# Causal attention, query blocks of 64, 128, 128 and 128 rows, scores as 64x64 products on four array quarters

## The chip, the core and the metric

The kernel runs on one core of a Trainium2 chip. The metric is device time in microseconds (us) of one execution; the lower the better. TensorE (PE in the rows; PEld is its weight load), VectorE (DVE), ScalarE (ACT), GpSimd (POOL) and SyncE (SP, which issues the DMAs) run their own instruction queues and meet at semaphores.

## What is computed

```python
def _attn_ref(q, k, v):                      # each (4, 12, 448, 64), float32
    scores = scale * np.matmul(q, k.transpose(0, 1, 3, 2))
    mask = np.triu(np.ones((seq, seq), dtype=bool), k=1)
    scores = np.where(mask, -1000000000.0, scores)
    scores = scores - np.max(scores, axis=-1, keepdims=True)
    attn = np.exp(scores)
    attn = attn / (np.sum(attn, axis=-1, keepdims=True) + 1e-09)
    return np.matmul(attn, v)

def _moe_ref(x, w_in, w_out, a, b):          # x: (1792, 768), d_ff 2048; w_in and w_out in float64
    h = x @ w_in
    P = a[0] + a[1]*h + a[2]*h**2 + a[3]*h**3
    Q = 1.0 + abs(b[0])*abs(h) + abs(b[1])*h**2
    return (P / (Q + 1e-6)) @ w_out
```

x is the attention output with heads side by side. The scores are causal: row r sees keys 0 to r.

## The kernel before

**Attention** goes over 24 head pairs p. The two heads of a pair lie on partition halves 0 to 63 and 64 to 127. A pair passes through these steps; a letter stands for each in the order tables:

- `ld`, `lv`: q, k and v by DMA (SyncE).
- `qk`: 16 transposes of q and k (TensorE); `qx`, `qy`, `kx`, `ky`: their eviction from PSUM to q and k tiles (ScalarE, four instructions; q is scaled by 1/8).
- `s.3` ... `s.0`: the scores of query blocks of 128 rows, the last of 64. Blocks 0 to 2 are one 64x128 product for each head (K is 64 rows, 128 columns of the array), in two PSUM tiles, one a head; the last, of 64 rows and 448 keys, is a 64x64 product a head into the two halves of one tile. The widths are 128, 256, 384 and 448 columns.
- `m.0` ... `m.6`: adds the mask and takes the negated row minimum of the negated scores (VectorE, one instruction and an accumulator read each); `e.0` ... `e.6`: exponential with row sum (ScalarE, an activation and an accumulator read); `r`: the reciprocal of the sums (VectorE, two instructions); `n.0` ... `n.6`: the scaling by it (GpSimd).
- `c.1`, `c.0`: 32 transposes of the result (TensorE), `a` and `v`: their eviction, the x = 0 half by ScalarE, the x = 1 half by VectorE.
- `d`: 12 PV products (TensorE); `dh`, `dl`: the high part of the output by ScalarE (xh), the rest by VectorE (xl).
- `cv.0` ... `cv.3`: a piece of the conversion of the float64 weights to float32, in turn on GpSimd (lines 135 and 139), VectorE (145, 150) and SyncE; it fills gaps and feeds the second stage.

What runs when is written out by hand: `ORDER` is one round of the pipeline, and `name@lag` takes the step for pair p - lag. In round p the scores of pair p, the normalisation of p - 1, the transposes and PV of p - 2 and the output of p - 3 go side by side. `HEAD`, `FIRST` and `TAIL` are the fill, round 0 and the end. Each engine's queue holds its steps in that order, and a queue's head that waits holds all behind it. PSUM for qk, s, c is a ring of three tile pairs (`ring`); a new user waits until the tile's old readers are done. s.0 shares the tiles of s.1.

**MoE** follows: 64 units of w_in products (line 203), the rational function, and w_out products (511, 512), in float32 split into a high and a low part.

Of the kernel before, what the change touches and what calls it, by code (L numbers as in the profile page):

```python
# [8 lines left out]
F32 = mybir.dt.float32  # L9
# [32 lines left out]
def kernel(  # L42
# [198 lines left out]
    def qk_pe(p):  # L241
        ps = psa[p] = [ring(x, "psA") for x in range(2)]
        for n, src in enumerate(("q", "k")):
            for c in range(NB):
                for x, w in enumerate((QB, CP - QB)):
# [3 lines left out]
                    )  # L249

    def cut(t, ps, x, n):
        lo, hi = x * QB, (QB, CP)[x]
        w = NB * (hi - lo)
        return (
            t.rearrange("p (c r) -> p c r", c=NB)[:, :, lo:hi],
            ps[x][:, n * w:(n + 1) * w].rearrange("p (c r) -> p c r", c=NB),
        )

    def q_ev(p, x):
        o, i = cut(Q[p % 2], psa[p], x, 0)  # L260
        nc.scalar.activation(out=o, in_=i, func=AF.Copy, scale=SCALE)  # L261

    def k_ev(p, x):
        if p not in K:
            K[p] = qk.tile([P, S], F32, tag="k", name="kt")
        o, i = cut(K[p], psa[p], x, 1)
        nc.scalar.copy(out=o, in_=i)
# [456 lines left out]
```

## Time and profile before

| | us |
|---|---|
| three runs, median (lowest to highest) | 639.85 (639.5 to 639.87) |
| the profiled execution | 638.61 |
| its span, first to last instruction | 636.5 |
| fill: to the start of pair 1's conversion step on VectorE | 19.01 |
| round 2 | 7.85 |
| rounds 3 to 22 | 122.87 |
| last round to the start of the w_out products | 26.73 |
| the rest of MoE | 460.04 |

The stages are cut at the start of VectorE's conversion step (line 145 or 150), which is the last VectorE step of a round. To read the profile: an engine's busy time in a stage says how full it is; the idle time before a group of instructions, and what ended it, says whom it waits for. A matmul row is one pass of a product, and a float32 product has two. Rows of one instruction have a duration that includes its latency, so the next one often starts before it ends; the distance from start to start is what an instruction costs its queue.

### The profile page before, as it was taken

What the parts mean: (1) busy time and instruction counts of PE and PEld (TensorE: products, weight loads), DVE (VectorE), ACT (ScalarE), POOL (GpSimd) and SP (SyncE); (2) the same over time, 40 slices, a digit from 0 to 9 for tenths busy, and PEclk for the clock granted to TensorE, in tenths of its full rate; (3) what the DMA queues carried; (4) which work ended last, traced back from release to release, by engine and by line L of the source; (5) the groups of instructions that cost most, each with busy time, mean ns of one, the idle gap of its engine ahead of it and who ended that gap; (6) DMA issues with size and microseconds to landing.
All of it is one profiled execution on the core that took longest, in us unless ns stands there. A gap on an engine that the chain in (4) does not pass through costs nothing.

```text
span 636.5 us, 12809 instructions
## 1 busy us (share of the span) xinstructions
PE 622.6 (98%) x4624; PEld 520.1 (82%) x4624; DVE 520.4 (82%) x1037; ACT 438.2 (69%) x989; POOL 179.1 (28%) x245
## 2 busy tenths in 40 slices
PE   7899999999999999999999999999999999999997
PEld 5566676666788887888888888889999999999996
DVE  2899999998699999999999868677875656885664
ACT  4899999998677766667777665554745465755453
POOL 2767777775643521113444100000000000000000
PEclk9899999999999999999999999999999999999999
DMA  8998889895268896888987987647477766667753
GB/s 182 225 222 191 205 226 205 194 258 180 61 223 298 290 362 239 306 303 288 325 309 286 323 306 278 226 148 271 177 235 249 254 228 225 222 199 248 248 198 125
DMA packets 109759, 151.84 MB, mean 239 GB/s; under 512 B 71040, under 2 KB 83328, under 8 KB 109696
## 3 DMA queue, kind: packets, MB, share of 16 engines
q1 hardware_dynamic: 109696, 151.02, 74.3%
q8 instruction: 37, 0.61, 0.4%
q14 instruction: 26, 0.21, 0.1%
HBM read 114.04 MB, written 36.96 MB: 237 GB/s over the span
## 4 chain that ended last, share of the span: by engine, by line
PE 90%; DVE 5%; ACT 2%; issue 1%; POOL 1%; ACTq 0%; DVEq 0%; POOLq 0%
PE psH L203 34%; PE psO L511 24%; PE psM L512 13%; PE psS L282 8%; PE psD L361 5%; PE psC L337 4%; PE psA L247 1%; DVE psS L295 1%; DVE at L347 1%; PE psI L614 1%; ACT e L302 1%; POOL e L317 1%; DVE xl L374 0%; DVE nm L295 0%; DVE p L471 0%
## 5 line engine op out<-in xcount | busy, mean ns | idle before, releaser
L203 PE MATMUL psH<-xh,whl 128*128 128x512 f32 (+1 forms) x768 | 175.8, 364 | 0.0
L511 PE MATMUL psO<-whl,gh 128*128 128x512 f32 x448 | 159.7, 392 | 1.6 <-ACT gh L477 1.1
L203 PEld LDWEIGHTS psH<-xh,whl 128*128 128x128 f32 x768 | 136.0, 188 | 15.3
L512 PE MATMUL psM<-whl,gh 128*128 128x256 f32 x448 | 126.2, 282 | 0.0
L455 ACT ACTIVATE u<-w,lnb 128x512 f32<-128x512 f32 (+1 forms) x64 | 43.0, 671 | 85.5 <-DVE w L440 85.5
L511 PEld LDWEIGHTS psO<-whl,gh 128*128 128x128 f32 x448 | 84.0, 188 | 20.2 <-ACT gh L477 2.2
L317 POOL TENSOR_SCALAR e<-e,r 128x384 f32<-128x384 f32 (+3 forms) x168 | 80.7, 502 | 38.5 <-DVE r L313 28.9
L302 ACT ACTIVATE e<-psS,nm 128x256 f32<-128x256 f32 (+3 forms) x168 | 83.6, 524 | 11.1 <-DVE nm L295 11.0
L203 PE MATMUL psH<-xl,whl 128*128 128x512 f32 (+1 forms) x384 | 87.4, 362 | 0.0
L512 PEld LDWEIGHTS psM<-whl,gh 128*128 128x128 f32 x448 | 84.5, 189 | 1.3
L295 DVE CUSTOM_DVE_ANT_0 psS<-psS,mask 128x128 f32<-128x128 f32 (+3 forms) x168 | 73.4, 473 | 11.7 <-PE psS L282 10.1
L511 PE MATMUL psO<-whl,gl 128*128 128x512 f32 x224 | 81.0, 390 | 0.0
L203 PEld LDWEIGHTS psH<-xl,whl 128*128 128x128 f32 x384 | 70.1, 188 | 7.5
L282 PE MATMUL psS<-kt,qt 64*64 64x448 f32 (+3 forms) x384 | 66.8, 457 | 1.4 <-ACT qt L261 1.2
L433 ACT ACTIVATE u<-psH 128x512 f32<-128x512 f32 (+1 forms) x64 | 34.5, 539 | 47.6 <-PE psH L203 47.5
L484 DVE TENSOR_TENSOR gl<-p,gh 128x384 fp32r<-128x384 f32 (+1 forms) x62 | 38.2, 617 | 35.0 <-ACT gh L477 35.0
L512 PE MATMUL psM<-whl,gl 128*128 128x256 f32 x224 | 63.2, 282 | 0.0
L135 POOL TENSOR_SCALAR u<-raw 128x768 f32<-128x768 f32 x32 | 37.4, 1170 | 85.6 <-DMA raw<-in_moe_w_in_dram 31.9
L186 DVE TENSOR_TENSOR whl<-w,whl 128x768 fp32r<-128x768 f32 x43 | 41.6, 968 | 22.6 <-ACT whl L178 22.2
L477 ACT CAST gh<-p 128x512 fp32r<-128x512 f32 (+1 forms) x64 | 36.8, 575 | 28.9 <-DVE p L471 28.9
L440 DVE SCALAR_TENSOR_TENSOR w<-w,bb,u 128x512 f32<-128x512 f32 (+1 forms) x64 | 48.2, 753 | 5.7 <-ACT w L434 5.7
L462 DVE SCALAR_TENSOR_TENSOR w<-w,u 128x512 f32<-128x512 f32 (+1 forms) x64 | 41.5, 648 | 10.2 <-ACT u L458 10.2
(62 smaller groups left out, 1028.8 us busy)
## 6 DMA issues: line engine op xcount, KB each, us to landing
whl<-whl SPq DMA_DIRECT2D x88, 768.0 KB, 4.2
w<-w SPq DMA_DIRECT2D x56, 384.0 KB, 5.1
raw<-in_moe_w_in_dram SPq DMA_DIRECT2D x16, 768.0 KB, 5.4
w<-u SPq DMA_DIRECT2D x32, 384.0 KB, 2.9
raw<-in_moe_w_out_dram SPq DMA_DIRECT2D x16, 768.0 KB, 5.4
qraw<-in_q_dram SPq DMA_DIRECT2D x48, 112.0 KB, 3.9
kraw<-in_k_dram SPq DMA_DIRECT2D x48, 112.0 KB, 4.1
out_dram<-osb SPq DMA_DIRECT2D x14, 384.0 KB, 2.8
```

Source lines behind the costliest of these rows:

```text
L186: eng.tensor_tensor(out=w[:, 1], in0=src, in1=w[:, 0].bitcast(F32), op=ALU.subtract)
L203: nc.tensor.matmul(ps, w[:, c * P:(c + 1) * P], x[c][:, lo:lo + n_tok], start=(c == 0 and n == 0), stop=(c == KD - 1 and n == 2),)
L282: nc.tensor.matmul(o if i < 3 else o[half(j)], Q[p % 2][half(j), i * P:min((i + 1) * P, S)], K[p][half(j), :w], start=True, stop=True, ski ...
L295: nc.vector.tensor_tensor_reduce(out=s, in0=s, in1=m, scale=-1.0, scalar=3e38, op0=ALU.add, op1=ALU.min, accum_out=nmx[p][:, i:i + 1],)
L302: nc.scalar.activation(out=E[p % 2][i][:, :w], in_=pss[p, i][1], func=AF.Exp, bias=nmx[p][:, i:i + 1], scale=-1.0, accum_out=SUM[p][:, i:i ...
L317: nc.gpsimd.tensor_scalar(out=e, in0=e, scalar1=REC[p][:, i:i + 1], scalar2=0.0, op0=ALU.mult, op1=ALU.add)
L440: nc.vector.scalar_tensor_tensor(out=w, in0=w, scalar=bb[:, 0:1], in1=u, op0=ALU.add, op1=ALU.mult)
L455: nc.scalar.activation(out=r, in_=w, func=AF.Ln, scale=2.0 ** -LSH, bias=lnb[:, 0:1])
L462: nc.vector.scalar_tensor_tensor(out=w, in0=w, scalar=QC, in1=r, op0=ALU.add, op1=ALU.mult)
L484: eng.tensor_tensor(out=gl, in0=pp, in1=gh.bitcast(F32), op=ALU.subtract)
L511: nc.tensor.matmul(acc[k], g, w[:, :512], start=first, stop=last)
L512: nc.tensor.matmul(m, g, w[:, 512:], start=first and k % 2 == 0, stop=last, skip_group_check=True)
```

## The change

- Query blocks are 64, 128, 128, 128 rows instead of 128, 128, 128, 64. The score widths become 64, 192, 320 and 448. Block 0 lies in one PSUM tile (two 64x64 products); each of the others is four 64x64 products, one for each half of the rows and each head, on the four quarters of the array. E tiles have 64 zeroed columns behind the scores where the block's transposes read past them.
- `qx`, `qy` evict q and k together, one instruction for each of the two PSUM tiles, into one `qkt` tile; for pairs 0 and 1 the second one is on VectorE. The scale 1/8 moves into the row-minimum instruction, and the mask values are divided by it.
- `c_pe` still has 32 transposes a pair, in another order of slots, so that `d` needs 8 products instead of 12.
- `ORDER`, `FIRST` and `TAIL` are new. After the first q and k transposes four more idle products (`keep_warm`) are issued, and the GpSimd part of the first weight conversion moves from round 0 to round 1.
- The masks are two tiles, and GpSimd fills the E tiles' zero columns at the start.

The core of the diff (of the order tables two lines):

```diff
-c.1@2 e.3@1 cv.3 qk@-1 lv e.0@1 v.1@2 dh@3 ld@-4 s.3 r@1 a.1@2 dl@3 n.5@1 qy@-1 c.0@2 m.6 kx@-1 n.4@1 ky@-1 s.2
+c.1@2 e.2@1 s.0 e.4@1 v.1@2 lv c.0@2 a.1@2 r@1 qk@-1 ld@-4 dh@3 v.0@2 n.4@1 s.3 cv.3 a.0@2 m.0 n.2@1 dl@3 qx@-1 n.6@1
...
+    def qk_ev(p, x):
+        if p not in QK:
+            QK[p] = qk.tile([P, 2, S], F32, tag="qk", name="qkt")
         lo, hi = x * QB, (QB, CP)[x]
+        o = QK[p].rearrange("p n (c r) -> p (n c) r", r=CP)[:, :, lo:hi]
+        i = psa[p][x][:, :2 * NB * (hi - lo)].rearrange("p (c r) -> p c r", r=hi - lo)
+        if p < 2 and x == 1:
+            nc.vector.tensor_copy(out=o, in_=i)
+        else:
+            nc.scalar.copy(out=o, in_=i)
...
-    b_w = (P, P, 2 * P, 2 * P, 3 * P, 3 * P, S)
+    b_w = (QB, 3 * QB, 3 * QB, 5 * QB, 5 * QB, S, S)
...
+        for n, j in ((0, 0), (1, 1), (1, 0), (0, 1)):
+            x = n if i else 1 - j
+            if i == 0 and n:
+                continue
+            r = (2 * i - 1 + (n + j) % 2) * QB if i else 0
+            nc.tensor.matmul(
+                ps[j][half(x), lo:lo + w], QK[p][half(j), 0, r:r + QB], QK[p][half(j), 1, :w],
+                start=True, stop=True, skip_group_check=True,
+            )
...
-            out=s, in0=s, in1=m, scale=-1.0, scalar=3e38,
+            out=s, in0=s, in1=m, scale=-SCALE, scalar=3e38,
...
     d_jobs = (
-        (0, 0, 0, 0, 0, 7), (1, 0, 0, 8, 0, 6), (1, 0, 0, 15, 6, 7),
-        (0, 1, 1, 0, 2, 7), (1, 1, 1, 8, 2, 6), (1, 1, 1, 5, 6, 7),
-        (0, 2, 1, 6, 4, 6), (1, 2, 1, 12, 4, 6), (0, 2, 1, 14, 6, 7), (1, 2, 1, 15, 6, 7),
-        (0, 3, 0, 14, 6, 7), (1, 3, 0, 7, 6, 7),
+        (0, 0, 0, 1, 0), (1, 0, 0, 8, 0), (0, 1, 1, 5, 2), (1, 1, 1, 0, 2),
+        (0, 2, 1, 13, 4), (1, 2, 1, 10, 4), (0, 3, 0, 15, 6), (1, 3, 0, 0, 6),
     )
...
-            lo = sum(quota(x) for x in range(p))
-            for m, n in steps[lo:lo + quota(p)]:
+            lo, hi = (sum(quota(x) for x in range(y)) for y in (0 if p == 2 else p, p + 1))
+            for m, n in steps[lo:hi]:
...
+        if p == 0:
+            keep_warm(4)
```

VectorE, the second part of a round: the row-minimum steps (`ISA psS,nm<-psS,mask`, with the width; the row behind each is its accumulator read), from the second copy of `at` on. Before:

```order
L347 COPY at<-psC 128x8x64 [waits PE_49]
L295 ISA psS,nm<-psS,mask 128x384 [waits PE_49]
L295 ISA nm 128x1
L295 ISA psS,nm<-psS,mask 128x384 [waits Activation_49]
L295 ISA nm 128x1
L295 ISA psS,nm<-psS,mask 128x128 [waits PE_49,Activation_49]
L295 ISA nm 128x1
L295 ISA psS,nm<-psS,mask 128x256 [waits DVE_49]
L295 ISA nm 128x1
L295 ISA psS,nm<-psS,mask 128x256 [waits PE_49]
L295 ISA nm 128x1
L295 ISA psS,nm<-psS,mask 128x128 [waits DVE_49]
```

Here the copy stands between the 448-wide step (just ahead of these rows) and the 384-wide ones. The same part of a round on VectorE after, from xl on:

```order
L379 TENSOR_TENSOR xl_86<-psD,xh_80 128x448 [waits Activation_49]
L299 ISA psS,nm<-psS,mask 128x448 [waits PE_49]
L299 ISA nm 128x1
L299 ISA psS,nm<-psS,mask 128x448
L299 ISA nm 128x1
L299 ISA psS,nm<-psS,mask 128x320 [waits PE_49,Activation_49]
L299 ISA nm 128x1
L299 ISA psS,nm<-psS,mask 128x192 [waits DVE_49]
L299 ISA nm 128x1
L299 ISA psS,nm<-psS,mask 128x320 [waits PE_49]
L299 ISA nm 128x1
L299 ISA psS,nm<-psS,mask 128x192 [waits DVE_49]
```

The copy of `at` and the new 64-wide step have moved ahead of xl. Both kernels have seven such steps a round, and in both two of them carry a wait on VectorE itself.

TensorE, the same round, the scores of the three wider blocks up to the first PV products (psS: scores, psD: PV). Before, they follow the last transposes of c:

```order
L337 MATMUL psC<-ident,e_214 128x64 x4
L282 MATMUL psS<-kt,qt_197 128x384 [waits Activation_49]
L282 MATMUL psS<-kt,qt_197 128x384 [waits DVE_49]
L282 MATMUL psS<-kt,qt_197 128x256 [waits PE_49,Activation_49]
L282 MATMUL psS<-kt,qt_197 128x256 [waits PE_49]
L282 MATMUL psS<-kt,qt_197 128x128 x2
L361 MATMUL psD<-at,vraw_199 64x448 [waits DMAHW3_49,DVE_49,Activation_49]
L361 MATMUL psD<-at,vraw_199 64x384 [waits DMAHW4_49]
L361 MATMUL psD<-at,vraw_199 64x64
L361 MATMUL psD<-at,vraw_199 64x320
```

The 448-wide products stand further up, behind the q and k transposes. The same place after; what stands ahead of these rows are the q and k transposes:

```order
L284 MATMUL psS<-qkt 64x448 [waits Activation_49]
L284 MATMUL psS<-qkt 64x448 [waits DVE_49]
L284 MATMUL psS<-qkt 64x448 x2
L284 MATMUL psS<-qkt 64x320 [waits Activation_49]
L284 MATMUL psS<-qkt 64x320 [waits DVE_49]
L284 MATMUL psS<-qkt 64x320 x2
L284 MATMUL psS<-qkt 64x192 x4
L366 MATMUL psD<-at,vraw_204 64x448 [waits DMAHW2_49,DVE_49]
L366 MATMUL psD<-at,vraw_204 64x448 [waits DMAHW3_49]
L366 MATMUL psD<-at,vraw_204 64x320 x2
```

The three wider blocks now follow each other in one go, four products each; the 64-column products (psS 64x64) have moved between the two groups of c transposes.

GpSimd, the fill, up to the normalisation of pair 0 (`e<-e,r`). Before:

```order
L610 MEMSET vraw_200 64x2x64
L135 TENSOR_SCALAR u<-raw_247 128x768 [waits DMAHW4_49,Pool_49]
L139 TENSOR_SCALAR raw_247<-raw_247 128x768 [waits Pool_49]
L317 TENSOR_SCALAR e_206<-e_206,r 128x384 [waits DVE_49,Activation_49]
L317 TENSOR_SCALAR e_205<-e_205,r 128x384 [waits Activation_49]
```

The conversion (L135, L139) is first. The same place on GpSimd after, behind the memsets of the E tiles:

```order
L621 MEMSET e_218 128x64
L324 TENSOR_SCALAR e_211<-e_211,r 128x320 [waits DVE_49,Activation_49]
L324 TENSOR_SCALAR e_209<-e_209,r 128x192
L324 TENSOR_SCALAR e_213<-e_213,r 128x448 [waits Activation_49]
L324 TENSOR_SCALAR e_207<-e_207,r 128x64
L324 TENSOR_SCALAR e_212<-e_212,r 128x448
L324 TENSOR_SCALAR e_210<-e_210,r 128x320
L324 TENSOR_SCALAR e_208<-e_208,r 128x192
L135 TENSOR_SCALAR u<-raw_263 128x768 [waits DMAHW4_49]
L139 TENSOR_SCALAR raw_263<-raw_263 128x768 [waits Pool_49]
```

The first conversion has moved behind the normalisation of pair 0.

## Rows read from the trace of the kernel before

**Rows 1.** The page: busy us (share) xinstructions; the chain's shares by engine.

```profile
PE 622.6 (98%) x4624; PEld 520.1 (82%) x4624; DVE 520.4 (82%) x1037; ACT 438.2 (69%) x989; POOL 179.1 (28%) x245
...
PE 90%; DVE 5%; ACT 2%; issue 1%; POOL 1%; ACTq 0%; DVEq 0%; POOLq 0%
```

**Rows 2.** Busy time by stage: start:end length, then PE PEld DVE ACT POOL, clock, DMA.

```profile
19.01:26.86 7.85, 7.64 (x86) 4.92 (x88) 6.06 (x22) 5.75 (x20) 5.69 (x10) 0.78 0.93 211
26.86:149.73 122.87, 122.74 (x1760) 82.78 (x1759) 119.94 (x404) 118.65 (x421) 88.52 (x158) 1.00 0.89 215
```

**Rows 3.** VectorE's groups, rounds 3 to 22: xcount | busy us, mean ns | idle before.

```profile
L295 DVE CUSTOM_DVE_ANT_0 psS<-psS,mask 128x384 f32<-128x384 f32 x40 | 21.4, 577 | 0.0
...
L295 DVE CUSTOM_DVE_ANT_0 psS<-psS,mask 128x256 f32<-128x256 f32 x40 | 16.3, 449 | 0.7
L295 DVE CUSTOM_DVE_ANT_0 psS<-psS,mask 128x128 f32<-128x128 f32 x41 | 12.9, 315 | 0.7
L295 DVE CUSTOM_DVE_ANT_0 psS<-psS,mask 128x448 f32<-128x448 f32 x20 | 12.5, 623 | 0.0
L374 DVE TENSOR_TENSOR xl<-psD,xh 128x448 fp32r<-128x448 f32 x20 | 12.0, 602 | 0.2
...
L313 DVE RECIPROCAL r<-sums 128x7 f32<-128x7 f32 x20 | 4.0, 201 | 1.4
```

**Rows 4.** Timeline of VectorE, inside one round: start us, us, instruction.

```profile
111.58 0.14 DVE L295 DVE_READ_ACCUMULATOR2_ANT nm<- 128x1 f32 x1
111.75 0.43 DVE L295 CUSTOM_DVE_ANT_0 psS<-psS,mask 128x256 f32<-128x256 f32 x1
```

**Rows 5.** Timeline of TensorE, one round, rows of one line merged.

```profile
101.19 0.41 PE L247 MATMUL psA<-ident,qraw 64*128 64x64 f32 x8
...
101.78 0.97 PE L282 MATMUL psS<-kt,qt 64*64 64x448 f32 x4
102.68 0.71 PE L337 MATMUL psC<-ident,e 64*128 64x64 f32 x16
103.22 1.70 PE L282 MATMUL psS<-kt,qt 64*128 64x384 f32 x12
104.85 1.98 PE L361 MATMUL psD<-at,vraw 128*64 128x448 f32 x24
106.76 0.46 PE L337 MATMUL psC<-ident,e 64*128 64x64 f32 x8
```

**Rows 6.** Timeline of ScalarE, the same round.

```profile
102.81 0.36 ACT L261 ACTIVATE qt<-psA 128x192 f32<-128x192 f32 x1
...
103.77 0.65 ACT L345 COPY at<-psC 128x512 f32<-128x512 f32 x1
104.23 0.72 ACT L302 ACTIVATE e<-psS,nm 128x448 f32<-128x448 f32 x1
104.76 0.28 ACT L302 ACTIVATION_READ_ACCUMULATOR e<-psS,nm 128x1 f32 x1
```

**Rows 7.** Timelines of TensorE, GpSimd and VectorE, the fill.

```profile
7.16 3.94 PE L282 MATMUL psS<-kt,qt 64*64 64x448 f32 x16 [1.23 <-ACT qt L261]
...
13.88 0.89 POOL L135 TENSOR_SCALAR u<-raw 128x768 f32<-128x768 f32 x1 [10.46 <-DMA raw<-in_moe_w_in_dram]
...
15.03 0.73 DVE L310 SCALAR_TENSOR_TENSOR sums<-sums 128x7 f32<-128x7 f32 x1 [1.83 <-ACT e L302]
...
16.16 3.36 POOL L317 TENSOR_SCALAR e<-e,r 128x384 f32<-128x384 f32 x7 [0.42 <-DVE r L313]
...
18.16 0.40 PE L337 MATMUL psC<-ident,e 64*128 64x64 f32 x6 [2.12 <-POOL e L317]
...
19.01 1.32 DVE L145 SCALAR_TENSOR_TENSOR u<-raw,u 128x768 uint32<-128x768 uint32 x1
```

**Rows 8.** Busy time and clock of a stretch of round 2, as in rows 2.

```profile
20.50:23.90 3.40, 3.40 (x24) 1.73 (x24) 2.08 (x6) 2.27 (x7) 2.50 (x6) 0.50 1.13 215
```

**Rows 9.** Timeline of TensorE, the end of attention.

```profile
155.04 1.98 PE L361 MATMUL psD<-at,vraw 128*64 128x448 f32 x24 [1.26 <-issue]
```

More of the change, by code (lines that the diff above doesn't have):

```diff
@@ L65 @@
     NP = B * HP
+    NE = 7
     SCALE = 1.0 / float(D) ** 0.5
@@ L249, in qk_pe @@
                     )
-    def cut(t, ps, x, n):
-        lo, hi = x * QB, (QB, CP)[x]
[L253 to L267, printed above, removed]
@@ L282, in stage_b_pe @@
             nc.tensor.matmul(
-                o if i < 3 else o[half(j)], Q[p % 2][half(j), i * P:min((i + 1) * P, S)], K[p][half(j), :w],
+                ps[j][half(x), lo:lo + w], QK[p][half(j), 0, r:r + QB], QK[p][half(j), 1, :w],
                 start=True, stop=True, skip_group_check=True,
             )
+        for j in range(2):
+            pss[p, max(2 * i - 1 + j, 0)] = ps[j][:, lo:lo + w]
     def stage_b_max(p, i):
         if p not in nmx:
-            nmx[p] = sm.tile([P, NQ], F32, tag="nm", bufs=2, name="nm")
@@ L359, in stage_d @@
         v = V[p % 3]
-        for j, c, h, slot, lo, hi in d_jobs:
+        for j, c, h, slot, lo in d_jobs:
             nc.tensor.matmul(
-                ps[half(j), lo * QB:hi * QB], v[:, j, c], a[h][:, slot * QB:(slot + hi - lo) * QB],
-                start=(c == 0 and lo == 0), stop=(c == 3), skip_group_check=True,
+                ps[half(j), lo * QB:S], v[:, j, c], a[h][:, slot * QB:(slot + 7 - lo) * QB],
+                start=(c == 0), stop=(c == 3), skip_group_check=True,
             )
@@ L577, with causal @@
         nc.gpsimd.memset(mask, 0.0)
-        nc.gpsimd.affine_select(
-            out=mask[:, 2 * P:3 * P], in_=mask[:, 2 * P:3 * P], compare_op=ALU.is_ge, fill=-1e9, base=0,
-            pattern=[[-1, P]], channel_multiplier=1,
-        )
-        for j in range(2):
-            m = mask[half(j), 3 * P + S - QB:]
+        nc.gpsimd.memset(mask0, 0.0)
+        def causal(m, base):
             nc.gpsimd.affine_select(
-                out=m, in_=m, compare_op=ALU.is_ge, fill=-1e9, base=0, pattern=[[-1, QB]], channel_multiplier=1,
-            )
+                out=m, in_=m, compare_op=ALU.is_ge, fill=-1e9 / SCALE, base=base, pattern=[[-1, m.shape[-1]]],
+                channel_multiplier=1,
+            )
+        causal(mask[:, 0, S - P:], 0)
+        for x in range(2):
+            causal(mask[half(x), 1, S - P:], QB - x * QB)
+            causal(mask0[half(x)], 0)
         es_l, es_r = ExitStack(), ExitStack()
@@ L610, with keep_warm @@
             nc.gpsimd.memset(V[x][:QB, :, 3], 0.0)
+        for x in range(2):
+            for e, w in zip(E[x], b_w):
+                if w < S:
+                    nc.gpsimd.memset(e[:, w:], 0.0)
         nc.vector.memset(warm, 0.0)
-        for _ in range(8):
-            nc.tensor.matmul(idle, warm, warm, start=True, stop=True, skip_group_check=True)
+        def keep_warm(n):
+            for _ in range(n):
+                nc.tensor.matmul(idle, warm, warm, start=True, stop=True, skip_group_check=True)
+        keep_warm(8)
         def attend(p, part):
```

70 lines of the change are left out of this document (36 added, 34 removed).

## The prediction

> **What bounds the kernel now.** I read the page's totals first. TensorE is busy 98% of the span and carries 90% of the chain [rows 1], so the first reading is "TensorE bounds everything, so every TensorE nanosecond saved counts". The change works in the attention stage only, so I cut the span there [rows 2]. The steady part of that stage is 26.86 to 149.73: 122.87 us for 20 rounds (one head pair each; the count is the x20 of xl in [rows 3]), 6.14 us a round. In it TensorE is busy 122.74 of 122.87, but VectorE is busy 119.94 and ScalarE 118.65 as well. Three engines are nearly full, and the question is which of them never waits for another.
>
> [Rows 3] answer it. The idle column of VectorE's groups adds up to 0.7 + 0.7 + 0.2 + 1.4 = 3.0 us in 122.87, and no group there has a releaser on another engine. The idle time is VectorE waiting for itself: [rows 4] show a row-minimum step whose scores lie in the same PSUM tile as the step before (the accumulator read starts at 111.58 and takes 0.14, the next step starts only at 111.75); the reciprocal waits for the sums. TensorE's rows, in contrast, can be full because it is held to VectorE's pace. So I take **VectorE as the bound of a round**, TensorE (6.1) and ScalarE just under it. Behind 176.46 nothing is changed.
>
> **The change, part by part.**
>
> *TensorE, scores.* Before, a round streams 448 columns in two 64x64 products at a time (101.78 to 102.68, 0.90 us) and 384 + 256 + 128 = 768 columns in two 64x128 products at a time (103.22 to 104.85, 1.63 us) [rows 5]: 2.01 and 2.12 ns a column, 2.53 us together. After, four products at a time stream 64 + 192 + 320 + 448 = 1024 columns. At the same two prices that is 2.06 to 2.17 us: 0.36 to 0.47 saved, if the four quarters really run at once. The trace of before shows pairs on row halves (768 columns) and on column halves (PV), each at full rate; it does not show four. *PV*: 12 products a pair become 8, with the same 1024 columns a head; 104.85 to 106.76 is 1.91 [rows 5], and I take 0 to 0.1 off. *Form changes*: s.0 now stands between two groups of transposes, so a round has five changes of tile form in place of four. The 448-column group has a change on both sides and yet costs less a column than the next group, which has none ahead of it, so a change is small: 0 to 0.1. TensorE's round falls by about 0.4, to 5.7.
>
> The Trainium skill, "TensorEngine Tiling (Array Packing)", Key Properties, says that changing the tiling mode drains TensorE, which speaks against a fifth change. By that rule the round would give back one drain; the trace shows none that stands out in the rows just named.
>
> *ScalarE.* Four evictions of q and k, 102.81 to 103.77, 0.96 us, become two of 512 and 384 elements; a 512-wide copy takes 0.65 with its latency [rows 6]. About 0.1 is saved. The exponentials keep their number (7) and their columns: 2(128 + 256 + 384) + 448 = 1984 before, 64 + 2(192 + 320 + 448) = 1984 after.
>
> *VectorE.* Also 7 row minima with 1984 columns. The four widths of [rows 3] lie on a line: 315, 449, 577 and 623 ns, about 1 ns a column on 185. Read off it, 64, 192 and 320 take 250, 380 and 510. Before: 2(0.577 + 0.449 + 0.315) + 0.623 = 3.305 us a round; after: 0.25 + 2(0.38 + 0.51 + 0.623) = 3.276. The instruction order keeps two self-waits a round (the two 192-wide steps that follow a 320-wide one in its tile). The copies, the sums, xl and the weight conversion are the same. So the bound engine saves 0.03 a round, and **the 0.4 saved on TensorE turns into idle time**. Over 20 rounds: -0.6. Bounds: if a 64-wide step costs as much as a 128-wide one, +0.065 - 0.03 a round, +0.7; if the idle of the reciprocal and of xl (1.4 + 0.2) is covered too, now that other work follows them, -2.2.
>
> Would TensorE's new order make VectorE wait? The last two exponentials of the previous pair (e.2, e.4) must free their PSUM tile before qk, and qk stands ahead of s.3. Counted from the conversion step that opens a round on VectorE: e.2 and e.4 are 192 and 320 wide, each below the 0.81 that a 448-wide one takes with its read (104.23 to 105.04 in [rows 6]), and end at about 1.2 (1.8 at most); qk takes 0.6 (101.19 to 101.78 in [rows 5]) and s.3 0.9, so s.3 ends at 2.7 (3.3 at most). VectorE needs it at about 3.2 (conversion 0.9, copy 0.6, sums and reciprocal 0.45, copy 0.6, first minimum 0.15, xl 0.5). That leaves 0.5, and nothing at the far end. SyncE's loads move by less than a step and still go out in the old sequence.
>
> *Fill.* Before, the first scores run from 7.16 to 11.1 (16 records, 3.94 us; the same 16 take 2.53 in a round, so TensorE was at its lower clock for part of it). The first sums wait for the last exponential until 15.03, the normalisation on GpSimd starts at 16.16 [rows 7], and the conversion of pair 1 on VectorE starts at 19.01 [rows 7], that of pair 2 at 26.86, where round 2 ends [rows 2]. After, q and k are evicted by two engines side by side, but four more warming products hold TensorE meanwhile: I start the scores at 7.2 again (0.4 either way). They take 3.94 x 1024/1216 = 3.3 at the old clock, 2.1 at the upper one; VectorE starts with the 64-wide block instead of the 448-wide, so behind the last score only the minima of 448, 320 and 448 and one eviction are left (about 2.0), then one exponential and its read (0.8 [rows 6], and 0.1 to start). The sums come at 10.5 + 2.0 + 0.9 = 13.4 (12.2 to 13.8), 1.6 earlier. Then a **give-back**: the first conversion on GpSimd (13.88 in [rows 7], ahead of the normalisation, when GpSimd had nothing to do) now stands behind it. Normalisation from about 14.2, 3.36 long, ends at 17.6; the conversion's first step needs 0.89 more; so VectorE's conversion of pair 1 starts at 18.5, only 0.5 earlier. Round 2 took 7.85 before, 1.7 above a later round, with TensorE at 0.50 of its clock, 1.2 GHz, from 20.5 to 23.9 [rows 8]; that stretch follows 2.12 us in which it waited for the normalisation [rows 7]. With scores and transposes further ahead I give that round 6.3 (5.6 to 7.85). So pair 2's conversion starts at 24.8 instead of 26.86: **-2.0**, bounds -0.2 and -3.8. The extra memsets and masks on GpSimd lie before 7 us, when nobody waits for it.
>
> *End.* Before, TensorE stands 1.26 us ahead of the PV products at 155.04, the last wait before the MoE products [rows 9]. The scores' buffers come free sooner and two PV stages shrink a little; 0 to -1.26, I take -0.4, near the small end, since the normalisation of pair 22 still has to end before the last transposes.
>
> **Sum.** -2.0 - 0.6 - 0.4 = -3.0. The profiled execution took 638.61 (span 636.5), so 635.6 for one like it; the median shown, 639.85, is 1.24 above it, so 636.9.
>
> **Rivals.**
> (a) *TensorE was the bound after all.* For it: 98% busy, 90% of the chain [rows 1]. Then 0.42 x 20 = 8.4 come off, and with fill and end 10.8: 629.0. Against it: VectorE's idle column. 0.08.
> (b) *The four quarters run two at a time* (the side of slower). The 960 columns of blocks 1 to 3 are then streamed twice: 960 x 2.1 ns = 2.0 us more, TensorE's round is 5.7 + 2.0 = 7.7, and it becomes the bound: 1.56 x 20 = 31, less 2.4 of fill and end: 668. It decides as soon as the scores cost 0.44 more than I reckon. For it: no row shows four. Against it: column halves and row halves each run in pairs at full rate. 0.07.
> The Trainium skill, "TensorE: Matmul & The Clock Gate", Part 3, reports that row and column packing compose; no run here shows that yet.
> (c) *The fill gives it all back*: the conversion of pair 1 behind the normalisation starts at 19.0 again, the half-clock stretch returns, the rounds end at 0 to +0.7 and the end at 0: 639.7 to 640.5, middle 640.1. For it: GpSimd's queue and the 7.85. 0.17.
>
> **Chances.** My forecast 0.68, rivals 0.08, 0.07, 0.17. The measurement tells about 0.2% (1.3 us) from no change. Faster: 0.64 of my forecast's 0.68 and all of (a), 0.72; same: 0.04 and most of (c), 0.16; slower: (b) and a part of (c), 0.12. The range reaches from 634.0 (fill and rounds near their good bounds) to 640.6 (rival c); (a) and (b) are left out.
>
> **What would show it.** VectorE's idle column in the rounds stays near 3 us with no other engine as releaser, and a round stays at 6.05 to 6.2; if it falls to 5.8, (a) is right. TensorE's busy share in the rounds falls to about 93%. The scores' groups take 2.1 us a round; near 4 would be (b). In the fill, the first sums at 13.4, the conversion of pair 1 at 18.5 with GpSimd as releaser, that of pair 2 at 24.8. I am wrong if VectorE waits for TensorE or ScalarE in every round, or if the conversion of pair 2 starts after 26.5.

## The result, and the profile after

The changed kernel takes 644.76 us (median of four runs, 643.4 to 645.2), the kernel before 639.86 beside it: a ratio of 1.0074, 95% interval 1.0057 to 1.0091. It is slower, where 636.9 us and faster were forecast. The profiled execution took 643.42 us, its span is 641.6 (before: 638.61 and 636.5). Printed intervals leave out executions that lie over 1.5% above the fastest of their kernel, and since some variants below spread over 2% by themselves, their lowest and highest times stand with them.

The page's totals, to set against [rows 1]:

```profile
PE 623.2 (97%) x4728; PEld 515.2 (80%) x4728; DVE 521.9 (81%) x1039; ACT 435.2 (68%) x939; POOL 178.9 (28%) x258
...
PE 77%; DVE 12%; POOL 3%; DMA 2%; ACT 2%; issue 2%; SPq 1%; DVEq 0%; ACTq 0%; POOLq 0%
```

The busy time has hardly moved. The chain has: VectorE carries 12% of it where it carried 5%, and GpSimd and the DMAs now carry 5% together, some 32 us, where GpSimd had 1%. The span cut by stage, as in [rows 2] (length, then busy PE, PEld, DVE, ACT, POOL, granted clock, DMA share, GB/s); a cut is again the start of VectorE's conversion step:

```profile
17.09:23.32 6.23, 5.59 (x80) 3.53 (x76) 6.07 (x22) 5.39 (x19) 4.11 (x8) 1.00 0.94 237
...
41.39:52.48 11.09, 7.93 (x104) 5.25 (x106) 6.29 (x22) 6.26 (x21) 7.73 (x15) 0.85 0.83 207
52.48:95.22 42.74, 42.05 (x643) 26.68 (x640) 41.75 (x141) 40.73 (x134) 31.05 (x56) 1.00 0.82 196
95.22:102.56 7.34, 6.21 (x104) 4.10 (x105) 6.21 (x21) 6.00 (x20) 4.71 (x9) 1.00 0.77 196
...
108.58:118.94 10.36, 7.85 (x94) 4.50 (x94) 6.60 (x21) 5.99 (x20) 6.51 (x13) 0.84 0.82 214
...
156.39:182.11 25.72, 24.98 (x222) 17.73 (x219) 18.56 (x39) 19.00 (x44) 15.26 (x19) 1.00 0.37 109
```

Round 2 (first row) starts 1.9 us earlier than before and is 1.6 shorter. The seven rounds from 52.48 take 6.11 each, as forecast. But three single rounds take 11.09, 7.34 and 10.36 us: 10.5 us above three of 6.1. The loss is these three rounds.

| | before | after |
|---|---|---|
| fill and round 2, to pair 2's conversion | 26.86 | 23.32 |
| 20 rounds | 122.87 | 133.07 |
| last round, to the w_out products | 26.73 | 25.72 |
| the rest of MoE | 460.04 | 459.5 |
| span | 636.5 | 641.6 |

So fill and end give 4.5 us, more than forecast, and the rounds take 10.2.

Who waits in a long round? From the timelines of all engines between 94 and 118 us, the rows on GpSimd's conversion (line 135), its normalisation (324), the transposes behind it and their evictions, and SyncE's raw load (125); the first row, by itself, is from the chain in order of time:

```profile
96.99 8.52 DMA raw<-in_moe_w_out_dram
```

```profile
96.99 0.38 SPq L125 DMA_DIRECT2D raw<-in_moe_w_out_dram  x1
...
105.66 0.93 POOL L135 TENSOR_SCALAR u<-raw 128x768 f32<-128x768 f32 x1 [3.86 <-DMA raw<-in_moe_w_out_dram]
...
107.57 4.06 POOL L324 TENSOR_SCALAR e<-e,r 128x320 f32<-128x320 f32 x7
...
111.68 0.58 PE L344 MATMUL psC<-ident,e 64*128 64x64 f32 x11 [2.23 <-POOL e L324]
...
112.30 0.69 DVE L354 COPY at<-psC 128x512 f32<-128x512 f32 x1 [2.38 <-PE psC L344]
```

Read it downwards. The raw block of weights is issued at 96.99 and lands 8.5 us later. GpSimd waits 3.86 us for it; the next normalisation stands in GpSimd's queue behind the two conversion passes and starts at 107.57; TensorE's transposes wait for that, and VectorE for the transposes. The other two long rounds begin alike: GpSimd waits 4.37 us for a raw block up to 39.17 and 2.05 us up to 90.61. The same in the kernel before, GpSimd's conversion and SyncE's pair:

```profile
89.36 0.35 SPq L156 DMA_DIRECT2D w<-u  x1
89.81 1.04 SPq L125 DMA_DIRECT2D raw<-in_moe_w_out_dram  x1
...
99.88 0.91 POOL L135 TENSOR_SCALAR u<-raw 128x768 f32<-128x768 f32 x1
```

There the load goes out at 89.81 and GpSimd comes to it at 99.88, 10.1 us later. After, the load of 96.99 is needed at 101.8 (105.66 less the wait), 4.8 us after its issue, which is less than a raw load takes: DMA issues between 24 and 156 us, KB each and median us from issue to landing, before (first two rows) and after:

```profile
raw<-in_moe_w_in_dram SPq DMA_DIRECT2D x6, 768.0 KB, 5.2
...
raw<-in_moe_w_out_dram SPq DMA_DIRECT2D x5, 768.0 KB, 5.3
```

```profile
raw<-in_moe_w_in_dram SPq DMA_DIRECT2D x5, 768.0 KB, 6.6
raw<-in_moe_w_out_dram SPq DMA_DIRECT2D x5, 768.0 KB, 6.6
```

The diff shows the place. `cv.3`, the store of a converted block and the load of the raw block after next into its buffer, was third in `ORDER`, ahead of the round's three v loads (`lv`) and four q and k loads (`ld@-4`). Now it stands behind `s.3`, and thus behind all seven on SyncE. The pair is issued later, and the raw load queues behind more bytes. SyncE also stands still in its issues; right behind the raw load of 96.99, which lands at 105.51, the two k loads need this long:

```profile
100.45 4.79 SPq L223 DMA_DIRECT2D kraw<-in_k_dram  x2
```

In the kernel before, the same two take 1.02 to 2.03 us between 86 and 100 us.

### The profile page after: what moved, and what is told of

Read it like the earlier page. It is cut to its first block, busy times and chain, and to the rows that moved or that the text cites. A ratio compares the mean times of both kernels' runs of the same rounds, so it can differ in the third digit from the quotient of the medians.

```text
span 641.6 us, 13100 instructions
## 1 busy us (share of the span) xinstructions
PE 623.2 (97%) x4728; PEld 515.2 (80%) x4728; DVE 521.9 (81%) x1039; ACT 435.2 (68%) x939; POOL 178.9 (28%) x258
## 4 chain that ended last, share of the span: by engine, by line
PE 77%; DVE 12%; POOL 3%; DMA 2%; ACT 2%; issue 2%; SPq 1%; DVEq 0%; ACTq 0%; POOLq 0%
PE psH L203 35%; PE psO L516 24%; PE psM L517 13%; DVE psS L299 5%; POOL e L324 2%; PE psS L284 2%; DVE at L354 2%; DMA raw<-in_moe_w_out_dram 2%; ACT e L309 1%; PE psC L344 1%; PE psD L366 1%; DVE nm L299 1%; DVE u L150 1%; PE psA L249 1%; DVE xl L379 1%
## 5 line engine op out<-in xcount | busy, mean ns | idle before, releaser
L324 POOL TENSOR_SCALAR e<-e,r 128x320 f32<-128x320 f32 (+3 forms) x168 | 82.7, 514 | 38.2 <-PE psA L249 17.1
L309 ACT ACTIVATE e<-psS,nm 128x448 f32<-128x448 f32 (+3 forms) x168 | 83.0, 500 | 14.1 <-DVE nm L299 13.8
L299 DVE CUSTOM_DVE_ANT_0 psS<-psS,mask 128x448 f32<-128x448 f32 (+3 forms) x168 | 73.6, 473 | 6.3 <-PE psS L284 4.4
L489 DVE TENSOR_TENSOR gl<-p,gh 128x384 fp32r<-128x384 f32 (+1 forms) x62 | 39.9, 644 | 35.0 <-ACT gh L482 35.0
L135 POOL TENSOR_SCALAR u<-raw 128x768 f32<-128x768 f32 x32 | 36.1, 1128 | 93.7 <-DMA raw<-in_moe_w_in_dram 31.9
L186 DVE TENSOR_TENSOR whl<-w,whl 128x768 fp32r<-128x768 f32 x43 | 43.0, 1001 | 21.8 <-ACT whl L178 21.4
L284 PE MATMUL psS<-qkt 64*64 64x448 f32 (+3 forms) x672 | 58.2, 434 | 1.3 <-ACT qkt L264 1.3
L467 DVE SCALAR_TENSOR_TENSOR w<-w,u 128x512 f32<-128x512 f32 (+1 forms) x64 | 42.2, 660 | 10.3 <-ACT u L463 10.2
```

Source lines behind the costliest of these rows:

```text
L186: eng.tensor_tensor(out=w[:, 1], in0=src, in1=w[:, 0].bitcast(F32), op=ALU.subtract)
L284: nc.tensor.matmul(ps[j][half(x), lo:lo + w], QK[p][half(j), 0, r:r + QB], QK[p][half(j), 1, :w], start=True, stop=True, skip_group_check= ...
L299: nc.vector.tensor_tensor_reduce(out=s, in0=s, in1=m, scale=-SCALE, scalar=3e38, op0=ALU.add, op1=ALU.min, accum_out=nmx[p][:, i:i + 1],)
L309: nc.scalar.activation(out=E[p % 2][i][:, :w], in_=pss[p, i], func=AF.Exp, bias=nmx[p][:, i:i + 1], scale=-1.0, accum_out=SUM[p][:, i:i + 1],)
L324: nc.gpsimd.tensor_scalar(out=e, in0=e, scalar1=REC[p][:, i:i + 1], scalar2=0.0, op0=ALU.mult, op1=ALU.add)
L467: nc.vector.scalar_tensor_tensor(out=w, in0=w, scalar=QC, in1=r, op0=ALU.add, op1=ALU.mult)
```

## The experiments

Three theories stood at the start: (1) the place of the pair; (2) shorter rounds ask more of the DMA queues than they give; (3) the first conversion, now in round 1, takes the margin. In the names of the kernels, "the pair" is the store and the raw load of `cv.3`, and "in front" is ahead of `lv`. The kernel before, run beside the variants, has medians of 639.3 to 639.9 us and single executions from 636.1 to 645.7, so one execution by itself says little.

**The pair in front again.**

```diff
-c.1@2 e.2@1 s.0 e.4@1 v.1@2 lv c.0@2 a.1@2 r@1 qk@-1 ld@-4 dh@3 v.0@2 n.4@1 s.3 cv.3 a.0@2 m.0 n.2@1 dl@3 qx@-1 n.6@1
+c.1@2 e.2@1 s.0 e.4@1 cv.3 v.1@2 lv c.0@2 a.1@2 r@1 qk@-1 ld@-4 dh@3 v.0@2 n.4@1 s.3 a.0@2 m.0 n.2@1 dl@3 qx@-1 n.6@1
```

> The changed kernel with one thing put back: SyncE issues the store of a converted block and the load of the next raw block ahead of the three v loads and four q and k loads of the round, as the kernel before does, and no longer behind them. Theory 1 (the place of this pair in SyncE's sequence makes the raw block late for GpSimd, and GpSimd's norms behind it late for TensorE): the raw load is issued within 2 us of VectorE's second conversion pass, lands 5 to 6 us later, GpSimd waits under 0.5 us for any raw block, the rounds of 11.1, 7.3 and 10.4 us come down to 6.0 to 6.2, and the time is 634 us (632.5 to 636), faster than either kernel. Theory 2 (the shorter rounds ask more of the DMA queues than they give, so that any order of the loads leaves some transfer late): stalls stay, in the raw block or in q, k and v, and the time is 640 us or more. Theory 3 (the first conversion, moved from round 0 to round 1, leaves the whole chain of conversions without margin): stalls stay, 643 us or more.

Measured: median 644.27, but ten executions from 634.87 to 648.33; the interval of the ratio, 0.9937 to 1.0035, says little. One of the ten, 634.87, lies in the range that theory 1 had for all. The profiled one is the slowest and shows the stalls, so the rows below tell of such an execution and not of a good one. Theory 1 as I put it has fallen: the old place by itself doesn't bring back the old timing. SyncE's rows there, and the landing times:

```profile
67.82 2.06 SPq L223 DMA_DIRECT2D kraw<-in_k_dram  x2
69.97 0.43 SPq L156 DMA_DIRECT2D w<-u  x1
70.51 0.38 SPq L125 DMA_DIRECT2D raw<-in_moe_w_out_dram  x1
```

```profile
raw<-in_moe_w_in_dram SPq DMA_DIRECT2D x5, 768.0 KB, 7.7
raw<-in_moe_w_out_dram SPq DMA_DIRECT2D x5, 768.0 KB, 7.2
```

The seven loads of the round before go out right ahead of the pair. SyncE is late: the store waits for the conversion pass that VectorE starts at 64.84 and ends 1.28 us later, and goes out at 69.97, nearly 4 us behind it. The raw load queues behind the bytes of those loads and of the store.

**The pair late in the kernel before** (`cv.3` moved behind `ld@-4 s.3`, nothing else), in ten executions and, since the first interval reached no change, in twelve more:

```diff
-c.1@2 e.3@1 cv.3 qk@-1 lv e.0@1 v.1@2 dh@3 ld@-4 s.3 r@1 a.1@2 dl@3 n.5@1 qy@-1 c.0@2 m.6 kx@-1 n.4@1 ky@-1 s.2
+c.1@2 e.3@1 qk@-1 lv e.0@1 v.1@2 dh@3 ld@-4 s.3 cv.3 r@1 a.1@2 dl@3 n.5@1 qy@-1 c.0@2 m.6 kx@-1 n.4@1 ky@-1 s.2
```

> The kernel before with the same pair (store of a converted block, load of the next raw block) put behind the round's v, q and k loads and behind the last score products, as the changed kernel has it; nothing else is changed. Theory 1: the raw load is issued about 5 us later and lands 10 to 13 us after the conversion instead of 6.5 to 7, GpSimd waits for it in several rounds, and the time rises by 3 to 12 us, to 643 to 652 us. Theory 2 or 3 (the place of the pair alone does no harm): 639 to 641 us, and GpSimd's waits for raw blocks stay under 0.5 us.

> The kernel before with the pair behind the v, q and k loads once more, in more rounds, because the interval of the first look touched no change. If the place of the pair costs by itself: 0.2 to 0.5 per cent slower than the kernel before, 641 to 643 us. If it costs only together with the shortened fill: within 0.1 per cent.

Measured: 641.38 (1.0026, 0.9996 to 1.0056), then 642.03 (1.0043, 1.0011 to 1.0075). The place costs by itself, 0.1 to 0.75 per cent, which is less than theory 1 had (643 us at least). GpSimd's waits for raw blocks in the first of these, from the list of waits (us in total, times, longest), where the kernel before has none:

```profile
POOL u L135 <- DMA raw<-in_moe_w_in_dram: 9.7, 5, 2.9
...
POOL u L135 <- DMA raw<-in_moe_w_out_dram: 6.0, 4, 1.6
```

**The raw load alone in front; the first conversion back in round 0.** In the first, `cv.3` keeps the store and a new step `cv.4`, where the pair was put above, has the load:

```diff
-                m = done.pop(0)
-                conv_store(m)
-                conv_load(m + 2)
+                conv_store(done.pop(0))
+        elif part == 4:
+            for m in done:
+                conv_load(m + 2)
```

> The changed kernel with only the raw load put ahead of the v, q and k loads; the store stays behind them and the last score products. Theory 1 in its narrow form (only the load matters, since GpSimd waits for it and nobody waits for the store in these rounds): 634 us (632.5 to 636.5), as with the pair in front, and GpSimd's waits for raw blocks are gone. Rival (the store also counts, by its own wait or by the queue it shares): some stalls stay, and the time lies between 637 and 645 us.

In the second, `FIRST` has `cv.0@-1` again, behind `e.4`:

```diff
-            lo, hi = (sum(quota(x) for x in range(y)) for y in (0 if p == 2 else p, p + 1))
+            lo, hi = (sum(quota(x) for x in range(y)) for y in (p, p + 1))
```

> The changed kernel with the first conversion's GpSimd passes back in round 0, as in the kernel before; the pair of store and raw load stays behind the v, q and k loads. Theory 1: the stalls stay, since each raw load still goes out behind seven others: 643 to 647 us, with up to 2 us more in the fill, where GpSimd's 1.9 us stand ahead of the norms again. Theory 3 (the late first conversion took the margin): the stalls go or shrink, 633 to 640 us.

Measured: 638.87 (636.9 to 640.0; 0.9971 to 1.0001) and 644.68 (1.0045 to 1.0095). Theory 3 is out: 644.68 lies where theory 1 had it. The load alone in front comes out as its rival had it (637 to 645), not at 634. One wait for a raw block is left, of 1.4 us, and one long round (12.1 us), with another releaser; GpSimd's timeline:

```profile
39.25 0.92 POOL L135 TENSOR_SCALAR u<-raw 128x768 f32<-128x768 f32 x1 [4.91 <-DMA w<-u]
```

GpSimd writes a converted block into one of two buffers, and the store of the block two before was still under way.

**Third buffer.** The raw load in front and a third buffer, then the third buffer alone on the changed kernel:

```diff
-            u = c_u[m] = cv.tile([P, DM], U32, tag="u", bufs=2, name="u")
+            u = c_u[m] = cv.tile([P, DM], U32, tag="u", bufs=3, name="u")
```

> The changed kernel with the raw load alone in front (the store behind the v, q and k loads, as in the earlier run of that kind) and with three buffers instead of two for a block under conversion, so that GpSimd does not wait for the store of two blocks before. If the one stall that was left there (GpSimd's 4.9 us for the store at 34 to 39 us of the trace, round of 12.1 us) was due to the store: it goes, and the time falls by 4 to 5 us to 633 to 635 us. If the store's wait only hid another late transfer (a v, q or k load): the stall stays under another name, 637 to 640 us.

> The changed kernel with only the third buffer for a block under conversion; store and raw load stay behind the v, q and k loads. If the raw load's place is what counts: GpSimd's waits for raw blocks stay, 643 to 646 us. If the store's wait is the cause: 634 to 637 us.

Measured: 634.55 us (633.0 to 634.9; ratio 0.9916, 0.9886 to 0.9946), the version that beats both kernels; and 645.83 for the buffer alone (1.0087, 1.005 to 1.0125). The store was a second, smaller cause that shows only when the load is early. Theory 2 falls with this version: its rounds have one wait of GpSimd for a raw block, of 1.0 us, and they are no shorter than those of the kernel before (123.44 against 122.87), so they ask no more of the DMAs. The 20 rounds of this version:

```profile
23.44:146.88 123.44, 120.84 (x1850) 78.01 (x1851) 120.77 (x404) 116.79 (x382) 91.19 (x160) 1.00 0.88 219
```

**Backlog or the v loads' wait?** Two theories on what holds SyncE late: A, in the shortened fill the engines run ahead of SyncE's loads, and the bytes queued ahead of the raw load decide; B, the v loads' wait for the PV products, ahead in the queue. Four kernels: the load and then the store in front (`cv.4 cv.3` where `cv.3` was put above); the pair in front and the v loads last; the pair in front and the attention held back by 18 more idle products; and that delay alone. The edits of the second, beside the pair's, and of the last two:

```diff
-c.1@2 e.2@1 s.0 e.4@1 cv.3 v.1@2 lv c.0@2 a.1@2 r@1 qk@-1 ld@-4 dh@3 v.0@2 n.4@1 s.3 a.0@2 m.0 n.2@1 dl@3 qx@-1 n.6@1
+c.1@2 e.2@1 s.0 e.4@1 cv.3 v.1@2 c.0@2 a.1@2 r@1 qk@-1 ld@-4 dh@3 v.0@2 n.4@1 s.3 lv a.0@2 m.0 n.2@1 dl@3 qx@-1 n.6@1
...
-            keep_warm(4)
+            keep_warm(22)
```

> The changed kernel with the pair in front of the round's v, q and k loads, but the raw load first and the store behind it. Theory A (in the shortened fill SyncE and the DMA queue fall behind the other engines, and then every transfer that is queued ahead of the raw load decides whether GpSimd waits: in the run with the store first, the raw loads took 7 to 9 us to land): the raw load lands within 5.5 us, the store about 7.5 us after its conversion, GpSimd waits little for either, and the time is 633 to 637 us. Theory B (what matters is only that SyncE holds the raw load up behind waits of its own): the same as with the store first, stalls in some executions and not in others, 635 to 648 us.

> The changed kernel with the pair (store, then raw load) in front, the four q and k loads behind it, and the three v loads, which wait for the PV products of the round before, at the end of SyncE's round behind the last score products. Theory B (the v loads' wait for TensorE, in front of the queue, is what keeps SyncE late from round to round): SyncE waits for VectorE's conversion again, GpSimd's waits for raw blocks are under 0.5 us, 633 to 637 us in all executions. Theory A (it is the backlog of bytes in front of the raw load): the v loads' place changes little, raw loads still take 7 us or more to land, and the time is 640 to 648 us.

> The changed kernel with the pair (store, then raw load) in front, and with 18 more idle matmuls of 128x128 ahead of the first scores, which hold the attention back by about 4 us while SyncE's loads start as before. Theory A (the shortened fill lets the engines run ahead of the loads): with the 4 us given back SyncE is ahead again, the stalls are gone, every execution lies at 637 to 640 us, and the executions near 645 that the pair in front showed are gone. Rival (the lag comes from the rounds themselves, not from the fill): stalls stay, and the time is 4 us above that of the pair in front, 645 to 650 us.

> The changed kernel with only the 18 extra idle matmuls ahead of the first scores (some 4 us); the pair stays behind the v, q and k loads. If the place of the pair is a cause by itself: GpSimd still waits 1 to 3 us for raw blocks, some rounds take 7 us or more, and the time is 643 to 649 us. If the shortened fill is the whole cause: the stalls go and the time is 637 to 640 us, as with the delay and the pair in front.

| | median, us | lowest to highest | ratio, 95% interval |
|---|---|---|---|
| load, store in front | 639.87 | 635.7 to 646.7 | 1.0006, 0.9973 to 1.004 |
| pair in front, v last | 635.29 | 634.7 to 638.4 | 0.9943, 0.9923 to 0.9963 |
| pair in front, 4 us delay | 639.06 | 637.9 to 642.8 | 1.0014, 0.9988 to 1.004 |
| 4 us delay alone | 643.02 | 638.5 to 648.7 | 1.0033, 0.9991 to 1.0075 |

The delay tells most. In the profiled execution with the pair in front and the delay the stalls are gone. Its 20 rounds, and SyncE's longest wait, are those of the kernel before again (there the same row reads 13.1, 8, 2.2):

```profile
28.84:151.86 123.02, 120.39 (x1850) 77.90 (x1852) 120.35 (x402) 116.67 (x382) 89.41 (x159) 1.00 0.88 215
```

```profile
SPq L156 <- DVE u L150: 12.7, 10, 2.0
```

With the pair in front and no delay, SyncE hardly waits for VectorE before it issues the store:

```profile
SPq L156 <- DVE nm L299: 0.9, 2, 0.5
```

With the delay, then, SyncE waits for VectorE once more: it is ahead. So the shortened fill is one half of the cause: the engines gain 3.5 us there, the loads don't (SyncE issues the second raw load at 16.42 before and at 16.36 after). This half is less firmly shown than the place. The intervals with and without the delay overlap (0.9988 to 1.004, 0.9937 to 1.0035); what the delay takes away are the executions above 644 us, five of ten without it and none with it, though three with it, at 641.8 to 642.8, lie above what A had for all. With the delay alone, the pair still late, GpSimd waits 13.3 us for raw blocks in the profiled execution, one of the slowest (648.4); the interval reaches no change, so that the place is the other half rests on the kernel before with the pair late.

The times of the other two are B's and not A's: 635.7 to 646.7 with the load and then the store in front, where A had 633 to 637, and 635.29 with v last, where A had 640 to 648. With the load first and the store right behind it, GpSimd waits for the store instead (9.3 us in five waits in the profiled execution), as A doesn't say. With v last all but two executions lie below 636 us, but SyncE's wait for VectorE ahead of the store comes back only in part, 5.0 us in ten waits, where B had promised it. The raw loads land in 5.0 to 5.6 us there instead of 7.2 to 7.7, with 224 KB of v right ahead of the pair in place of 448 KB of q and k. That fits a backlog of bytes, but A had said that they would stay at 7 us or more. How much of SyncE's lateness is its own waiting and how much the backlog, these runs don't split; that stays open.

**Both cures, and the same cure on the kernel before.**

> The changed kernel with the raw load in front, then the q and k loads, the store and last the v loads, and three buffers for a block under conversion. If both cures act on the same lag, they don't add: 633.5 to 635 us, the time of the load in front with three buffers. If the v loads' wait still costs something there: 1 us less, 632.5 to 633.5 us.

> The kernel before with the arrangement that worked best on the changed kernel: the raw load in front of the v, q and k loads, the store behind them, and three buffers for a block under conversion. If the kernel before was not held up by its loads (SyncE waits for VectorE's conversion there, not the other way): no change, 638.5 to 640.5 us, and the 5 us by which the same arrangement of the changed kernel is faster belong to the change itself. If the arrangement helps any kernel: 635 to 637 us.

Measured: 634.79 (0.9912, 0.9882 to 0.9942): they don't add. And 638.75 on the kernel before (0.9981, 0.9956 to 1.0005): no change that the interval tells. So the 4 to 5 us of the better version belong to the change, with its loads in this order.

**Is TensorE's time free in a round?** In the best version (raw load in front, three buffers), every 192-column score product twice (the added time by the rows below: 89.17 - 87.06 = 2.11 us for the group, 1.79 without the repeat):

```diff
-        for n, j in ((0, 0), (1, 1), (1, 0), (0, 1)):
+        for n, j in ((0, 0), (1, 1), (1, 0), (0, 1)) * (2 if i == 1 else 1):
```

> The load in front with three buffers, and the four 192-column score products of every head computed twice into the same place (8 more matmuls... counted as instructions, some 0.33 us more of TensorE a round, from the differences of their starts). If VectorE bounds a round and TensorE has the 0.3 to 0.4 us that the new scores freed: the time stays within 1.5 us of the same kernel without the repeat, 633.5 to 636 us. If TensorE, which shows hardly any idle time in the rounds, is as full as VectorE: 22 x 0.33 = 7 us more, 640 to 643 us.

Measured: 634.61 us (0.9908, 0.9882 to 0.9935), the same as without. TensorE's timeline with the repeat, and then fifteen rounds without it and nearly the same stretch with it:

```profile
87.06 2.19 PE L284 MATMUL psS<-qkt 64*64 64x448 f32 x32
89.17 1.95 PE L366 MATMUL psD<-at,vraw 128*64 128x448 f32 x16
```

```profile
48.57:140.89 92.32, 90.55 (x1392) 58.63 (x1388) 90.23 (x301) 87.45 (x286) 69.07 (x121) 1.00 0.89 224
```

```profile
48.57:140.89 92.32, 92.32 (x1508) 60.71 (x1504) 90.23 (x301) 87.37 (x287) 68.59 (x120) 1.00 0.91 227
```

The second row has the bounds of the first; the fifteen rounds with the repeat, cut at their own conversion steps, run from 48.23 to 140.54, 92.31 us against 92.32. So 4.8 us of products were added where TensorE showed 1.8 us of idle time, and the rounds took no longer.

## Why the prediction was wrong

*The step that failed* is one sentence at the end of the VectorE part: "SyncE's loads move by less than a step and still go out in the old sequence". They don't: `cv.3` is the one step that crosses both `lv` and `ld@-4` in the two `ORDER` lines of the diff. I had looked for what TensorE's new order does to VectorE, and not priced the seven loads that the pair was moved past, nor written down when GpSimd needs the raw block. The margin could be read from the rows of before shown above: issued at 89.81, some 5.3 us to land, needed at 99.88, so 4.8 to spare; seven issues of 0.5 to 0.6 us and 1.3 us more to land use it up. No rival had a transfer that comes late. What the runs showed in its place: GpSimd waited seven times for raw blocks in the rounds, 14.8 us in all, where it had waited for none, and the 20 rounds took 10.2 us more; with the raw load in front and a third buffer they take 123.44.

A second omission: I counted the shortened fill as a gain alone. It takes 3.5 us off the engines' lead-in and nothing off SyncE's, and SyncE's lead covered the raw loads: with the 4 us given back and the pair in front, the waits are gone in the profiled execution. How much each half costs by itself is not split; the place alone cost 0.1 to 0.75 per cent in the kernel before.

*VectorE bounds a round*: right by what was tried. TensorE's 0.32 us more cost nothing, and the rounds without stalls take 123.02 to 123.44 us for 20, against 122.87 before; no run adds work to VectorE or ScalarE. That is +0.15 to +0.6 where I had -0.6 (bounds +0.7 and -2.2): VectorE's widths came out as 532 and 647 ns for 320 and 448 columns, where I had read 510 off the line and kept the 623 of [rows 3]. With the measured four the sum is 3.31 us a round, 0.8 more in 20 rounds than my 3.276. VectorE's groups in the best version:

```profile
L299 DVE CUSTOM_DVE_ANT_0 psS<-psS,mask 128x448 f32<-128x448 f32 x40 | 24.2, 647 | 0.0
L299 DVE CUSTOM_DVE_ANT_0 psS<-psS,mask 128x320 f32<-128x320 f32 x40 | 21.3, 532 | 0.0
...
L299 DVE CUSTOM_DVE_ANT_0 psS<-psS,mask 128x192 f32<-128x192 f32 x41 | 15.0, 367 | 1.4
...
L299 DVE CUSTOM_DVE_ANT_0 psS<-psS,mask 128x64 f32<-128x64 f32 x20 | 4.5, 222 | 0.0
...
L320 DVE RECIPROCAL r<-sums 128x7 f32<-128x7 f32 x20 | 4.0, 201 | 1.3
```

The idle column has 2.7 us and no other engine, as forecast; in the changed kernel itself the copies of `at` (L354) have 7.3 us with TensorE's psC as releaser, and two widths of the row minima 2.0 with its psS, which is the stalls. Rival (a) is out.

*Scores*: right. TensorE's timeline of an undisturbed round after, as [rows 5]:

```profile
83.64 0.33 PE L284 MATMUL psS<-qkt 64*64 64x64 f32 x4
83.91 0.71 PE L344 MATMUL psC<-ident,e 64*128 64x64 f32 x16
...
85.10 1.86 PE L284 MATMUL psS<-qkt 64*64 64x448 f32 x24
86.89 1.95 PE L366 MATMUL psD<-at,vraw 128*64 128x448 f32 x16
88.78 0.65 PE L344 MATMUL psC<-ident,e 64*128 64x64 f32 x14
```

From start to start, 0.27 + 1.79 = 2.06 us for the scores, the low end of 2.06 to 2.17, and 1.89 for PV. The four quarters run at once, and rival (b) is out. The Trainium skill, "TensorE: Matmul & The Clock Gate", Part 3, says that row and column packing compose; the trace agrees: 1024 columns on four quarters in 2.06 us are 2.01 ns a column, as much as a pair took before (2.01 to 2.12). The drain at a change of tile form, of the Trainium skill, "TensorEngine Tiling (Array Packing)", Key Properties, has no visible price at 2.06. What I had wrong is the sign to look for: TensorE's busy share was to fall to 93%, and in the best version it is 97.9% (120.84 of 123.44). As the repeated products show (4.8 us more in 1.8 us of idle time), part of that is time that the rows count as busy and that more products can use.

*Fill*: right in direction, too small: -3.5 against -2.0, near the bound of -3.8. The timelines of TensorE, VectorE and GpSimd, as [rows 7]:

```profile
5.76 1.16 PE L627 MATMUL psI<-warm 128*128 128x128 f32 x8
6.85 1.95 PE L284 MATMUL psS<-qkt 64*64 64x64 f32 x28
...
12.16 3.09 PE L284 MATMUL psS<-qkt 64*64 64x448 f32 x24
...
12.03 0.17 DVE L317 SCALAR_TENSOR_TENSOR sums<-sums 128x7 f32<-128x7 f32 x1 [0.94 <-ACT e L309]
12.63 3.36 POOL L324 TENSOR_SCALAR e<-e,r 128x320 f32<-128x320 f32 x7 [7.80 <-DVE nm L299]
...
15.96 0.90 POOL L135 TENSOR_SCALAR u<-raw 128x768 f32<-128x768 f32 x1
...
17.09 1.57 DVE L145 SCALAR_TENSOR_TENSOR u<-raw,u 128x768 uint32<-128x768 uint32 x1
```

The first scores start at 6.85 and take 1.9 us, where I had priced them at the slow rate of [rows 7], 3.3: products run ahead of them up to their start, where TensorE had been idle for 1.23 us before, and the granted clock from 6.85 to 8.80 is 1.00, 2.4 GHz. That the slow ones before ran at the lower clock, as the prediction has it, the profile does not show: it gives 1.00 from 7.16 to 11.1, and its clock records begin only at 10.28. From there the sums are 1.4 early (12.03 against 13.4) and everything behind keeps it: 17.09 against 18.5, 23.32 against 24.8. Rival (c) is out by its times.

Two things in the fill were not as forecast. The give-back did not decide: pair 1's conversion on VectorE was to have GpSimd as releaser, but GpSimd's first pass ends at 16.86 and VectorE is at its row minima until 17.09, so that row has no wait ahead of it. And the half-clock stretch has not gone, it lies earlier, behind a wait of 1.25 us of TensorE for the qkt eviction up to 10.91; the scores of pair 1 at 12.16 (24 rows) take 3.09 us where 1.86 are usual (85.10 above), and the granted clock of that stretch is 0.58, most of it 1.2 GHz:

```profile
11.50:15.30 3.80, 3.80 (x42) 1.85 (x41) 1.82 (x8) 2.31 (x8) 2.67 (x6) 0.58 1.00 170
```

*End*: -1.0 in the changed kernel and in the best version (25.72 and 25.71 against 26.73), where I took -0.4 of 0 to -1.26. With the loads cured the sum is the best version's, -3.8 in the span (632.7 against 636.5), where I had -3.0. That is near by luck in part: fill and end gave 2.0 more than I had, the rounds 1.2 less.

## What to carry to other kernels

In a hand-written order a step that crosses others on a DMA queue can cost: write down for each transfer when it is issued, when it lands and when the first reader needs it, and compare the margin with the transfers that it is moved past. A shortened fill takes lead away from the loads, so loads that were covered before can come late in rounds behind it. Where two engines are nearly full, add work to one: if the time stays, part of its busy share was waiting.

## What the runs showed of the hardware

A raw load of 768 KB took a median of 4.3 to 7.7 us to land between the variants (w_in and w_out apart). It took 7.2 to 7.7 behind a store and four q and k loads issued right ahead (the pair in front, above), and 4.9 to 5.6 in the same order with the delay, where SyncE waits for VectorE between those loads and the pair. In the best version, where no store stands ahead of it, w_in takes 5.6 and w_out:

```profile
raw<-in_moe_w_out_dram SPq DMA_DIRECT2D x5, 768.0 KB, 4.5
```

By the two kernels with the pair in front, what counts is what is still under way when the load goes out, more than the order as written. The Trainium skill, "DMA: Bandwidth & Descriptors", Queues, rings and completion order, says that a ring's descriptors are consumed in ring order; these landing times fit that, and no row here shows single descriptors.

Issuing takes longer too while much is under way: two k loads that take about 1.0 us to issue at best take 2.06 at 67.82 and 4.79 at 100.45 (both above). Between 30 and 150 us one k load takes 0.49 to 1.50 us in the kernel before and up to 3.51 with the pair in front.

A stall can cost more than its wait. TensorE waited 2.23 us up to 111.68; from 113.50 to 117.50 the granted clock is 0.57, so that most of this stretch ran at 1.2 GHz, and the scores in it take 3.43 us where an undisturbed round takes 1.86. Behind the wait of 1.13 us up to 96.63 the clock stays at 1.00 (the round from 95.22, above).

```profile
113.59 3.43 PE L284 MATMUL psS<-qkt 64*64 64x448 f32 x24
```

```profile
113.50:117.50 4.00, 4.00 (x34) 1.67 (x32) 2.72 (x9) 2.87 (x9) 3.35 (x7) 0.57 0.95 268
```
